# Loading the sampled blocks of V with plain transfers on SyncE instead of GpSimd's indirect gathers, in a block-sparse attention with feed-forward layer

## The chip, the cores and the metric

The kernel runs on one core of a Trainium2 chip. The core has five engines with an instruction stream each: TensorE (PE; its weight loads are listed apart as PEld), VectorE (DVE), ScalarE (ACT), GpSimd (POOL) and SyncE (SP), which here only issues transfers. Sixteen DMA engines move the data between the device's memory (HBM) and the core's memory (SBUF). A transfer is issued by SP or ACT (a plain one) or by POOL (here: an indirect one, whose rows are given by a list of indices in SBUF). The metric is the device time of one execution in microseconds (us), as a median of several runs.

## What is computed

Attention over 4 batches, 8 heads, 768 positions and head size 64, followed by a feed-forward layer with softplus. The positions are cut into 24 blocks of 32. A query block sees its own key block and the two beside it, the first and the last block, and three sampled blocks that are given as data; the first and the last query block see everything.

```
blk_i, blk_j = pos[:, None] // 32, pos[None, :] // 32
mask = np.abs(blk_i - blk_j) <= 1
mask |= (blk_i == 0) | (blk_j == 0) | (blk_i == 23) | (blk_j == 23)
for qb in range(24):
    for kb in sampled_blocks[qb]:
        mask[qb*32:(qb+1)*32, kb*32:(kb+1)*32] = True
scores = np.where(mask, scale * q @ k.T, -1e9)
x = softmax(scores) @ v
h = x @ w_in
out = softplus(h) @ w_out
```

The sampled blocks are the same for all batches and heads.

## The kernel before

Each batch has six sets of query blocks. A set is four query blocks (two in the last), worked on in two units of four heads each; one more set per batch, the whole one, holds the first and the last query block, which see all keys. The sets go through the stages scores (L581), exponents (L642), transposes (L661), values (L682), normalise, turn, x_high and x_low. The pieces of three neighbouring units are interleaved (L768).

For the values of a set, `load_values` (L533) fills one of two buffers `vbuf` ("vg" in the profile). SP loads the neighbouring blocks of all query blocks with one transfer (L549) and, where the first and last block aren't in the buffer yet, those too (L558, L561). The three sampled blocks of each query block are one indirect transfer on POOL (L567): 96 rows of 512 floats, chosen by a column of the index table `ix`. There are 22 such gathers per batch, 88 in all. A set's gathers aren't issued at once: they are put on the list `value_work`, and `gather` (L460) takes one from it, and one from the list `key_work`, after every piece of attention; `gathered` empties the list of what a set needs before its value products.

The sampled key blocks take another way. The keys of a batch stand in SBUF, and POOL (for the very first set DVE and ACT) copies each sampled block to its place at an address from a register (L511). Its number comes out of a register into which the packed block numbers `pk` have been read (`registers`, L451; the read is L454). `pk` holds three numbers of five bits per query block, two query blocks to a 32-bit word.

At the start DVE makes the index table and the packed numbers from the sampled blocks (`make_index` L385 with the conversions L386 and L387, L391 and L396, then `pack_blocks` L375 to L383), then the mask. PE runs 100 warm-up matmuls (L831) meanwhile.

The order of instructions: SP's is that of the program, word for word. DVE's is so while `make_index` to the first keys are traced, POOL's for the first gathers. All else is ordered by a planner from estimated costs, except single instructions that are kept behind everything traced before them on their engine, such as ACT's two steps on each half of the weights (L155, L159).

Other things on SP, in its order around `load_values`: the queries of a set two further on (`load_queries`, L447, "qc"); the halves of the feed-forward weights as 64-bit numbers (L148, "raw"), which ACT (L155, L159), DVE (L165, L172, L178) and POOL (L182) turn into 32-bit floats; those halves that don't stay in SBUF, written back (L201, "wD"); the attention's result for the second pass over the layer (L766, "xD") and the partial results of the first pass (L317, "yD"); the keys of the next batch (L431, "kT").

In the program's text the start is: block numbers, queries 0, keys 0, warm-up, index and mask, queries 1, values of set 0, values of set 1, queries 2, the first three halves of the weights. The feed-forward matmuls (L237 to L239 and L295 to L297) of the first pass fill PE beside the attention from the fourth set on; those of the second pass come after it.

Of the kernel before, what the change touches and what calls it, by code (L numbers as in the profile page):

```python
# [8 lines left out]
F32 = mybir.dt.float32  # L9
F32R = mybir.dt.float32r  # L10
I32 = mybir.dt.int32
# [4 lines left out]
ALU = mybir.AluOpType  # L16
# [3 lines left out]
BLOCK = 32  # L20
# [30 lines left out]
def sparse_attention_ffn(  # L51
# [22 lines left out]
    nc = tc.nc  # L74
    B, NG, P, NP, NI, _ = q.shape
    NB = k.shape[2]
    S = NB * BLOCK
    LAST = NB - 1
# [7 lines left out]
    NR = 3  # L86
# [243 lines left out]
    ac = actx.enter_context(tc.tile_pool(name="ac", bufs=1, side="right"))  # L330
# [4 lines left out]
    rf = ac.tile([P, NB, NR], F32, name="rf")  # L335
    pkf = ac.tile([1, NB], F32, name="pkf")
    pk = ac.tile([1, NB - 2], I16, name="pk")
    pk32 = pk.bitcast(I32)
    io = ac.tile([NR * BLOCK, 1], I32, name="io")
    first = ac.tile([P, 1], I32, name="first")  # L340
    iof = ac.tile([NR * BLOCK, 1], F32, name="iof")
    ixf = ac.tile([NR * BLOCK, NB], F32, name="ixf")
    ix = ac.tile([NR * BLOCK, B, NB], I32, name="ix")
    mask = ac.tile([P, NG, NS], F32, name="mask")
    iu = ac.tile([P, NG], I32, name="iu")
    iuf = ac.tile([P, NG], F32, name="iuf")
# [5 lines left out]
    for i in range(NI):  # L352
        nc.gpsimd.iota(
            iu[i * BLOCK : (i + 1) * BLOCK], pattern=[[NI, NG]], base=1 + i, channel_multiplier=0
        )
    for s in range(NR):
        nc.gpsimd.iota(io[s * BLOCK : (s + 1) * BLOCK], pattern=[[0, 1]], base=0, channel_multiplier=1)
    for rows in (slice(0, NR * BLOCK), slice(NR * BLOCK, P)):
        nc.gpsimd.iota(first[rows], pattern=[[0, 1]], base=0, channel_multiplier=1)
    vbuf = [ac.tile([P, 2, NI, DM], F32, name=f"vg{n}") for n in range(2)]  # L360
# [2 lines left out]
        out=vbuf[0][:, 0, 0, :], out_offset=None, in_=v,  # L363
        in_offset=bass.IndirectOffsetOnAxis(ap=first, axis=0),
# [17 lines left out]
        )  # L382
        nc.vector.tensor_copy(out=pk, in_=pkf[:, 1 : NB - 1])  # L383

    def make_index():  # L385
        nc.vector.tensor_copy(out=iof, in_=io)  # L386
        nc.vector.tensor_copy(out=rf, in_=blk.rearrange("p (i s w) -> p i s w", s=NR, w=2)[:, :, :, 0])  # L387

        for s in range(NR):
            rows = slice(s * BLOCK, (s + 1) * BLOCK)  # L390
            nc.vector.tensor_scalar(  # L391
                out=ixf[rows], in0=rf[rows, :, s], scalar1=float(BLOCK), scalar2=iof[rows, 0:1],
                op0=ALU.mult, op1=ALU.add,
            )
        for b in range(B):
            nc.vector.tensor_scalar_add(out=ix[:, b], in0=ixf, scalar1=float(b * S))  # L396

    def make_mask():
        nc.vector.tensor_copy(out=iuf, in_=iu)
# [51 lines left out]
    def registers(eng, us):  # L451
        for u in us:
            if (eng, u) not in regs:
                regs[eng, u] = eng.value_load(pk32[0:1, u : u + 1], min_val=0, max_val=(1 << 31) - 1)  # L454
        return [regs[eng, u] for u in us]


    key_work, value_work = [], []

    def gather():  # L460
        for work in (value_work, key_work):
            if work:
                work.pop(0)[1]()

    def gathered(work, m):
        while work and work[0][0] <= m:
            work.pop(0)[1]()
# [17 lines left out]
    def gather_keys(m):  # L485
        b, g = order[m]
        ni = NI if g < NG - 1 else 2
        kd = kg[m % 2]

        def of_block(i):  # L490

            eng = (nc.vector if i < 2 else nc.scalar) if m == 0 else nc.gpsimd
            copy = nc.scalar.copy if m == 0 and i >= 2 else eng.tensor_copy
            if i == 0:
                at = kT[b][:, 4 * g : 4 * g + NR, :]
                pattern = [list(x) for x in at.ap]
                ins = nc.vector.tensor_copy(
                    out=kd[:, 0:ni, 0:NR, :].rearrange("p i s f -> p i (s f)"),
                    in_=bass.AP(at.tensor, at.offset, [pattern[0], [NP * BLOCK, ni], [1, NR * NP * BLOCK]]),
                )  # L500
                tc.keep_in_program_order(ins)
                if m % NG < 2:
                    first = nc.vector.tensor_copy if m == 0 else nc.scalar.copy
                    end_keys(m, (first, nc.scalar.copy))
            (r,) = registers(eng, [2 * g + i // 2])
            for s in range(NR):
                x = nc.s_assert_within(
                    eng.snap((r >> (16 * (i % 2) + 5 * s)) & 31), 0, LAST,
                    skip_runtime_bounds_check_because="a sampled block is one of the key blocks",
                )  # L510
                copy(  # L511
                    out=kd[:, i, 1 + NR + s, :], in_=kT[b][:, bass.ds(x, 1), :].rearrange("p n f -> p (n f)")
                )

        key_work.extend((m, lambda i=i: of_block(i)) for i in range(ni))


# [15 lines left out]
    def load_values(m):  # L533
        if m >= len(sets):
            return
        b, g, whole = sets[m]
        vd = vg[sets[m]] = vbuf[m % 2]
        if whole:
            rows = vd.rearrange("p c i f -> p (c i) f")
            for n in range(0, NCH, 2):  # L540
                lo = b * S + n * P
                nc.sync.dma_start(
                    out=rows[:, n : n + 2], in_=v[lo : lo + 2 * P].rearrange("(t p) f -> p t f", p=P)
                )
            return
        ni = NI if g < NG - 1 else 2

        i0 = 1 if m == 0 else 0
        nc.sync.dma_start(  # L549
            out=vd[0 : 3 * BLOCK, 0, i0:ni], in_=overlapping(v, b * S + (4 * g + i0) * BLOCK, ni - i0, 3 * BLOCK)  # L550
        )
        if g < 2:

            for c, lo in enumerate((b * S, (b + 1) * S - BLOCK)):
                i1 = i0 if c == 0 else 0
                if m < SPREAD:
                    if i1 == 0:
                        nc.sync.dma_start(out=vd[3 * BLOCK : P, c, 0], in_=v[lo : lo + BLOCK])  # L558
                    spread.append((vd[3 * BLOCK : P, c, 0:1], vd[3 * BLOCK : P, c, 1:]))
                    continue  # L560
                nc.sync.dma_start(  # L561
                    out=vd[3 * BLOCK : P, c, i1:],
                    in_=v[lo : lo + BLOCK].unsqueeze(1).to_broadcast([BLOCK, NI - i1, DM]),
                )

        def of_block(i):
            nc.gpsimd.indirect_dma_start(  # L567
                out=vd[0 : 3 * BLOCK, 1, i, :],
                out_offset=None,
                in_=v,  # L570
                in_offset=bass.IndirectOffsetOnAxis(ap=ix[:, b, 4 * g + 1 + i : 4 * g + 2 + i], axis=0),
            )

        value_work.extend((m, lambda i=i: of_block(i)) for i in range(ni))


    units = [(m, a) for m in range(len(sets)) for a in range(NA)]
# [104 lines left out]
    def values(n):  # L682
        m, a = units[n]
        b, g, whole = sets[m]
        pt = state[n]["pt"]
        gathered(value_work, m)
        vd = vg[sets[m]]
        if a == 0:
            xps[m] = ps_x.tile([P, DM], F32, tag="x", name=f"x{n}")
        xq = xps[m]  # L690

        if not whole:
            ni = NI if g < NG - 1 else 2
            for j in range(2):
                for r in range(2):
                    h = 2 * (2 * a + j) + r
                    for c in range(2):
                        for i in range(ni):
                            rows = slice(i * BLOCK, (i + 1) * BLOCK)
                            nc.tensor.matmul(  # L700
                                xq[rows, h * D : (h + 1) * D],
                                pt[r, 2 * j + c][:, rows],
                                vd[:, c, i, h * D : (h + 1) * D],
                                start=(c == 0), stop=(c == 1),
                            )
        else:
            rows_v = vd.rearrange("p c i f -> p (c i) f")
            for r in range(2):
                at = (2 * a + r) * D
                for c in range(NCH):  # L710
                    for o in range(2):
                        rows = slice(64 * o, 64 * o + 64)
                        h = 2 * (2 * a + o) + r
                        nc.tensor.matmul(  # L714
                            xq[rows, at : at + D],
                            pt[r, c][:, rows],
                            rows_v[:, c, h * D : (h + 1) * D],
                            start=(c == 0), stop=(c == NCH - 1),
                        )
# [110 lines left out]
    for n in range(WARM):  # L830
        nc.tensor.matmul(warm[:, n % 4], ident, ident, start=True, stop=True)  # L831
    with tc.manual_schedule(engines={mybir.EngineType.DVE}):
        make_index()
        pack_blocks()
        make_mask()
        load_keys(0)
        gathered(key_work, 0)
# [2 lines left out]
    load_keys(1)  # L840
    scores(0)
    with tc.manual_schedule(engines={mybir.EngineType.Pool}):
        gathered(value_work, 0)
        gathered(key_work, 1)
    spread_ends()
    load_values(1)
# [69 lines left out]
    for j in range(len(seq) + LEAD):  # L916
        if j >= SECOND:
            t, f = seq[j][1:] if j < len(seq) else (NTB, -1)
# [62 lines left out]
```

## Time and profile before

| What | Value |
|---|---|
| Median of 3 runs | 808.4 us (807.98 to 809.11) |
| Profiled execution, first to last instruction | 812.1 us |
| PE busy | 781.7 us |
| DVE busy | 574.8 us |
| ACT busy | 489.6 us |
| POOL busy | 223.3 us |
| Mean granted clock of PE | 0.989 |
| Bytes moved by DMA | 129.65 MB, of these 17.57 MB on POOL's queue |

The profile gives the span from the first to the last instruction of one execution; no other time is given for that execution. The span is 3.7 us longer than the median of the runs without a profile. "Idle before, releaser" is the time an engine stood before an instruction and what ended it; "issue" means that nothing in the profile explains it. SPq, ACTq, DVEq and POOLq are the instruction queues of the engines: transfers, register operations and semaphores, which aren't counted as busy. In a timeline a row is start, duration, engine, line, operation, destination and source, and how many instructions were merged.

### The profile page before, as it was taken

What the parts mean: (1) busy time and instruction counts of PE and PEld (TensorE: products, weight loads), DVE (VectorE), ACT (ScalarE), POOL (GpSimd) and SP (SyncE); (2) the same over time, 40 slices, a digit from 0 to 9 for tenths busy, and PEclk for the clock granted to TensorE, in tenths of its full rate; (3) what the DMA queues carried; (4) which work ended last, traced back from release to release, by engine and by line L of the source; (5) the groups of instructions that cost most, each with busy time, mean ns of one, the idle gap of its engine ahead of it and who ended that gap; (6) DMA issues with size and microseconds to landing.
All of it is one profiled execution on the core that took longest, in us unless ns stands there. A gap on an engine that the chain in (4) does not pass through costs nothing.

```text
span 812.1 us, 21433 instructions
## 1 busy us (share of the span) xinstructions
PE 781.7 (96%) x8108; PEld 647.6 (80%) x8108; DVE 574.8 (71%) x1474; ACT 489.6 (60%) x1182; POOL 223.3 (27%) x389
## 2 busy tenths in 40 slices
PE   8878898999999999999999999999999999999997
PEld 8545676877677777778778988999988999988996
DVE  5778999876887777886655985656565656656564
ACT  5878785757767767767565764444444444444442
POOL 6864775635565436563000000000000000000000
PEclk9999898999999999999999999999999999999999
DMA  8899678687696777866425640304040312122021
GB/s 254 241 257 336 171 212 266 195 294 247 184 291 198 248 261 200 267 171 184 158 78 182 250 178 20 137 1 155 2 146 10 116 40 105 52 88 68 0 79 40
DMA packets 48408, 129.65 MB, mean 160 GB/s; under 512 B 5489, under 2 KB 5617, under 8 KB 46257
## 3 DMA queue, kind: packets, MB, share of 16 engines
q1 hardware_dynamic: 42304, 109.79, 42.3%
q0 software_dynamic: 5712, 17.57, 7.6%
q8 instruction: 64, 1.05, 0.5%
q10 hardware_dynamic: 288, 0.93, 0.3%
q14 instruction: 40, 0.32, 0.1%
HBM read 97.85 MB, written 30.41 MB: 158 GB/s over the span
## 4 chain that ended last, share of the span: by engine, by line
PE 82%; DVE 7%; ACT 6%; DMA 2%; issue 2%; POOL 0%; SPq 0%; ACTq 0%; DVEq 0%; POOLq 0%
PE o L295 11%; PE h L237 11%; PE o L297 10%; PE o L296 10%; PE h L238 10%; PE h L239 10%; PE s L601 5%; PE t L670 4%; PE x L700 4%; ACT pr L657 3%; PE warm L831 2%; DMA kT<-in_k_dram 1%; PE s L625 1%; DVE pr L607 1%; PE x L714 1%
## 5 line engine op out<-in xcount | busy, mean ns | idle before, releaser
L237 PE MATMUL h<-x,w 128*128 128x384 f32 x512 | 180.0, 352 | 0.4 <-DVE nmax L632 0.2
L238 PE MATMUL h<-x,w 128*128 128x384 f32 x512 | 173.7, 339 | 0.0
L239 PE MATMUL h<-x,w 128*128 128x384 f32 x512 | 173.1, 338 | 0.0
L250 DVE TENSOR_SCALAR u<-e 128x384 f32<-128x384 f32 x128 | 50.8, 397 | 155.8 <-ACT e L244 154.4
L295 PE MATMUL o<-w,gh 128*128 128x512 f32 x384 | 158.7, 413 | 0.0
L657 ACT ACTIVATE pr<-pr,nmax 128x256 f32<-128x256 f32 (+2 forms) x208 | 110.4, 532 | 74.6 <-DVE nmax L607 60.4
L297 PE MATMUL o<-w,gl 128*128 128x512 f32 x384 | 152.0, 396 | 1.2 <-issue 1.0
L296 PE MATMUL o<-w,gh 128*128 128x512 f32 x384 | 151.7, 395 | 0.0
L243 ACT ACTIVATE e<-h 128x384 f32<-128x384 f32 x128 | 62.4, 487 | 114.9 <-PE h L239 114.8
L267 ACT CAST gh<-u 128x384 fp32r<-128x384 f32 x128 | 65.6, 513 | 79.2 <-PE o L296 78.1
L237 PEld LDWEIGHTS h<-x,w 128*128 128x128 f32 x512 | 96.6, 189 | 19.4 <-issue 11.2
L567 POOL DMA_INDIRECT vg<-in_v_dram,ix x88 | 90.3, 1027 | 65.9 <-PE x L700 39.1
L238 PEld LDWEIGHTS h<-x,w 128*128 128x128 f32 x512 | 96.8, 189 | 6.5 <-issue 2.2
L511 POOL COPY kg<-kT 128x128 f32 x252 | 86.0, 389 | 41.2 <-PE s L601 38.8
L239 PEld LDWEIGHTS h<-x,w 128*128 128x128 f32 x512 | 96.6, 189 | 0.0
L295 PEld LDWEIGHTS o<-w,gh 128*128 128x128 f32 x384 | 72.0, 188 | 19.9 <-issue 7.1
L297 PEld LDWEIGHTS o<-w,gl 128*128 128x128 f32 x384 | 72.1, 188 | 18.8 <-issue 1.5
L296 PEld LDWEIGHTS o<-w,gh 128*128 128x128 f32 x384 | 72.2, 188 | 10.3 <-issue 0.4
L607 DVE CUSTOM_DVE_ANT_1 pr<-s,mask 128x256 f32<-128x256 f32 (+1 forms) x192 | 69.6, 414 | 14.5 <-PE s L601 14.5
L258 ACT ACTIVATE u<-u 128x384 f32<-128x384 f32 x128 | 66.9, 523 | 15.4 <-DVE e L252 15.2
L263 DVE TENSOR_TENSOR u<-u,e 128x384 f32<-128x384 f32 x128 | 73.6, 575 | 3.0 <-ACT u L258 2.4
L273 DVE TENSOR_TENSOR gl<-u,gh 128x384 fp32r<-128x384 f32 x128 | 73.0, 570 | 2.8 <-ACT gh L267 2.8
(81 smaller groups left out, 1088.6 us busy)
## 6 DMA issues: line engine op xcount, KB each, us to landing
vg<-in_v_dram SPq DMA_DIRECT2D x19, 768.0 KB, 5.8
xD<-x SPq DMA_DIRECT2D x8, 1536.0 KB, 7.4
x<-xD SPq DMA_DIRECT2D x8, 1536.0 KB
raw<-in_w_in_dram SPq DMA_DIRECT2D x16, 512.0 KB, 9.3
raw<-in_w_out_dram SPq DMA_DIRECT2D x16, 512.0 KB, 8.3
qc<-in_q_dram SPq DMA_DIRECT2D x24, 256.0 KB, 6.9
vg<-in_v_dram SPq DMA_DIRECT2D x12, 512.0 KB, 7.4
yD<-os SPq DMA_DIRECT2D x24, 256.0 KB, 2.5
```

What stands on the lines that cost most here:

```text
L237: nc.tensor.matmul(ph, wh[:, cols], hi[:, c], start=(c == 0), stop=False)
L238: nc.tensor.matmul(ph, wh[:, cols], lo[:, c], start=False, stop=False)
L239: nc.tensor.matmul(ph, wl[:, cols], hi[:, c], start=False, stop=(c == NC - 1))
L263: nc.vector.tensor_tensor(out=l, in0=l, in1=e, op=ALU.add)
L273: nc.vector.tensor_tensor(out=gl, in0=l, in1=G[n].bitcast(F32), op=ALU.subtract)
L295: nc.tensor.matmul(po[m], gh[:, cols], wh, start=first, stop=False)
L296: nc.tensor.matmul(po[m], gh[:, cols], wl, start=False, stop=False)
L297: nc.tensor.matmul(po[m], gl[:, cols], wh, start=False, stop=last)
L511: copy(out=kd[:, i, 1 + NR + s, :], in_=kT[b][:, bass.ds(x, 1), :].rearrange("p n f -> p (n f)"))
L567: nc.gpsimd.indirect_dma_start(out=vd[0 : 3 * BLOCK, 1, i, :], out_offset=None, in_=v, in_offset=bass.IndirectOffsetOnAxis(ap=ix[:, b, 4 * ...
L607: nc.vector.tensor_tensor_reduce(out=pr[r][rows, j], in0=ps[r][rows, j], in1=mask[rows, g].unsqueeze(2).to_broadcast([ni * BLOCK, NS, BLOCK]),
L657: nc.scalar.activation(x, x, AF.Exp, bias=nmax[rows, r, j : j + 1], scale=-1.0, accum_out=rs[rows, h : h + 1])
```

## The change

Each sampled block of V is loaded by SP as a plain transfer of 32 rows of 512 floats (64 KB, contiguous in HBM), at an address that SP works out in registers from the packed block numbers. Three transfers per query block take the place of one gather: 264 for 88. They are issued in `load_values` itself, right behind the set's other loads, and are no longer spread over the pieces of attention. SP reads `pk` into registers (11 reads, at the first use of each). The index table, its tiles and the instructions that made it are gone; `make_index` becomes `read_blocks`, and only converts the block numbers. The extraction of a block number from its word is now one function for keys and values.

```
-    for s in range(NR):
-        nc.gpsimd.iota(io[s * BLOCK : (s + 1) * BLOCK], pattern=[[0, 1]], base=0, channel_multiplier=1)
...
-    def make_index():
-        nc.vector.tensor_copy(out=iof, in_=io)
+    def read_blocks():
         nc.vector.tensor_copy(out=rf, in_=blk.rearrange("p (i s w) -> p i s w", s=NR, w=2)[:, :, :, 0])
-
-        for s in range(NR):
-            rows = slice(s * BLOCK, (s + 1) * BLOCK)
-            nc.vector.tensor_scalar(
-                out=ixf[rows], in0=rf[rows, :, s], scalar1=float(BLOCK), scalar2=iof[rows, 0:1],
-                op0=ALU.mult, op1=ALU.add,
-            )
-        for b in range(B):
-            nc.vector.tensor_scalar_add(out=ix[:, b], in0=ixf, scalar1=float(b * S))
...
+    def sampled(eng, r, i, s):
+        return nc.s_assert_within(
+            eng.snap((r >> (16 * (i % 2) + 5 * s)) & 31), 0, LAST,
+            skip_runtime_bounds_check_because="a sampled block is one of the key blocks",
+        )
+
+    v_blocks = v.rearrange("(n p) f -> n p f", p=BLOCK)
...
     def gather():
-        for work in (value_work, key_work):
-            if work:
-                work.pop(0)[1]()
+        if key_work:
+            key_work.pop(0)[1]()
...
-        def of_block(i):
-            nc.gpsimd.indirect_dma_start(
-                out=vd[0 : 3 * BLOCK, 1, i, :],
-                out_offset=None,
-                in_=v,
-                in_offset=bass.IndirectOffsetOnAxis(ap=ix[:, b, 4 * g + 1 + i : 4 * g + 2 + i], axis=0),
-            )
-
-        value_work.extend((m, lambda i=i: of_block(i)) for i in range(ni))
+        for i in range(ni):
+            (r,) = registers(nc.sync, [2 * g + i // 2])
+            for s in range(NR):
+                nc.sync.dma_start(
+                    out=vd[s * BLOCK : (s + 1) * BLOCK, 1, i, :],
+                    in_=v_blocks[bass.ds(sampled(nc.sync, r, i, s) + b * NB, 1)].rearrange("n p f -> (n p) f"),
+                )
...
-        gathered(value_work, m)
```

More of the change, by code (lines that the diff above doesn't have):

```diff
@@ L338, in sparse_attention_ffn @@
     pk32 = pk.bitcast(I32)
-    io = ac.tile([NR * BLOCK, 1], I32, name="io")
     first = ac.tile([P, 1], I32, name="first")
-    iof = ac.tile([NR * BLOCK, 1], F32, name="iof")
-    ixf = ac.tile([NR * BLOCK, NB], F32, name="ixf")
-    ix = ac.tile([NR * BLOCK, B, NB], I32, name="ix")
     mask = ac.tile([P, NG, NS], F32, name="mask")
@@ L455, in registers @@
         return [regs[eng, u] for u in us]
-    key_work, value_work = [], []
+    def sampled(eng, r, i, s):
[4 more added lines that the diff above has]
+    v_blocks = v.rearrange("(n p) f -> n p f", p=BLOCK)
+    key_work = []
     def gather():
-        for work in (value_work, key_work):
-            if work:
-                work.pop(0)[1]()
+        if key_work:
+            key_work.pop(0)[1]()
     def gathered(work, m):
@@ L506, in of_block @@
             for s in range(NR):
-                x = nc.s_assert_within(
-                    eng.snap((r >> (16 * (i % 2) + 5 * s)) & 31), 0, LAST,
-                    skip_runtime_bounds_check_because="a sampled block is one of the key blocks",
-                )
+                x = sampled(eng, r, i, s)
                 copy(
@@ L564, in load_values @@
                 )
-        def of_block(i):
-            nc.gpsimd.indirect_dma_start(
-                out=vd[0 : 3 * BLOCK, 1, i, :],
-                out_offset=None,
-                in_=v,
-                in_offset=bass.IndirectOffsetOnAxis(ap=ix[:, b, 4 * g + 1 + i : 4 * g + 2 + i], axis=0),
-            )
-        value_work.extend((m, lambda i=i: of_block(i)) for i in range(ni))
+        for i in range(ni):
[5 more added lines that the diff above has]
+                )
     units = [(m, a) for m in range(len(sets)) for a in range(NA)]
@@ L832, in sparse_attention_ffn @@
     with tc.manual_schedule(engines={mybir.EngineType.DVE}):
-        make_index()
+        read_blocks()
         pack_blocks()
@@ L842, in sparse_attention_ffn @@
     with tc.manual_schedule(engines={mybir.EngineType.Pool}):
-        gathered(value_work, 0)
         gathered(key_work, 1)
```

## The prediction

> **What bounds the kernel now.** I read the windows first, to see in which stage TensorE (PE) has idle time at all, then the waits of PE, then the timelines of SP, ACT and PE where the idle time is.
>
> ```profile
> PE 781.7 (96%) x8108; PEld 647.6 (80%) x8108; DVE 574.8 (71%) x1474; ACT 489.6 (60%) x1182; POOL 223.3 (27%) x389
> 15.00:60.00 45.00, 35.12 (x856) 23.55 (x855) 33.13 (x112) 37.33 (x103) 35.23 (x67) 0.96 0.92 249
> 60.00:140.00 80.00, 69.85 (x995) 51.15 (x995) 75.05 (x187) 59.13 (x152) 50.73 (x73) 0.91 0.83 254
> 140.00:480.00 340.00, 335.27 (x4537) 264.45 (x4536) 258.96 (x724) 235.70 (x610) 128.17 (x221) 1.00 0.67 211
> 480.00:812.10 332.10, 327.94 (x1633) 294.92 (x1631) 199.51 (x410) 151.99 (x309) 0.00 (x0) 1.00 0.20 68
> ```
>
> Each window row gives its length, then busy us of PE, weight loads, DVE, ACT and POOL, the granted clock, the DMA share and GB/s. From 140 us on PE is idle for only 4.7 of 340 us and 4.2 of 332 us, at a granted clock of 1.00: it is the bound there, and what goes on beside it costs nothing unless it is later than PE's order allows. In the first 140 us PE is idle for 9.9 and 10.2 us of the two early windows. There the chain of work runs through ACT and DVE, and DMA is 0.92 and 0.83 busy. So the change is decided in the first sets of attention, and by whether anything becomes late afterwards.
>
> How much of PE's idle time do the gathers cause today?
>
> ```profile
> L567 POOL DMA_INDIRECT vg<-in_v_dram,ix x88 | 90.3, 1027 | 65.9 <-PE x L700 39.1
>   DMA vg<-in_v_dram,ix: 2.4, 4
> PEld s L601 <- POOL kg L511: 0.5, 2, 0.4
> 43.02 0.42 PE L700 MATMUL x<-vg,pt 128*32 128x64 f32 x12
> 43.92 0.30 PE L700 MATMUL x<-vg,pt 128*32 128x64 f32 x2 [0.48 <-DMA vg<-in_v_dram,ix]
> 44.75 0.97 PE L700 MATMUL x<-vg,pt 128*32 128x64 f32 x50 [0.53 <-DMA vg<-in_v_dram,ix]
> ```
>
> The gathers take 90.3 us of POOL, but POOL is busy for 27% of the span. The value products wait 2.4 us for gathers in all (weight loads and matmuls counted each, so about 1.2 us of real time: the pauses of 0.48 and 0.53 us at 43 to 45 us are nearly all of it). The scores wait 0.5 us for key copies on POOL. What can be won directly is thus 1.7 us.
>
> **The change part by part.** *Removed:* 88 gathers on POOL: 90.3 us of an engine off the path; worth the 1.2 + 0.5 us above. Eight small DVE instructions of the index:
>
> ```profile
> 6.63 0.71 DVE L391 TENSOR_SCALAR ixf<-rf,iof 32x24 f32<-32x24 f32 x3
> 7.37 0.42 DVE L396 TENSOR_SCALAR ix<-ixf 96x24 int32<-96x24 f32 x4
> 8.12 0.17 DVE L383 CAST pk<-pkf 1x22 int16<-1x22 f32 x1
> 1.45 14.28 PE L831 MATMUL warm<-ident 128*128 128x128 f32 x100 [1.45 <-POOL ident masks.py:199]
> ```
>
> They bring the packed block numbers `pk` from 8.29 to about 7.2 us, and everything behind them on DVE forward by 1.1 us. PE is in its warm-up until 15.73 us, which hides this: 0. Without that cover it would be worth the 1.1 us.
>
> *Added:* 264 transfers of 64 KB on SP, three per query block, with their register work, and a read of `pk` on SP.
>
> ```profile
> 189.11 1.75 SPq L431 DMA_DIRECT2D kT<-in_k_dram  x4
> L558 SPq DMA_DIRECT2D vg<-in_v_dram x3: 322/322/802, 2.8 to 10.1; - x3
> L511 ACTq ALU_OP  x11: 38/38/44, 12.2 to 13.4; - x11
> L511 ACTq FUSED_REGOPS  x6: 46/46/52, 12.3 to 13.5; - x6
> L454 ACTq TENSOR_LOAD <-pk x1: 473/473/473, 11.4 to 11.4; - x1
> L454 POOLq TENSOR_LOAD <-pk x11: 283/291/499, 8.3 to 21.8; - x11
> out_dram<-y SPq DMA_DIRECT2D x4, 64.0 KB, 2.1
> SPq L558 <- DMA kT<-in_k_dram: 3.9, 1, 3.9
> ```
>
> No transfer with a register address stands in this trace. SP issues four plain ones in 1.75 us, 0.44 us each. The key copies get their block number by two register operations of 38 ns and one of 46 ns; batches after the first add one more of 38 ns. That makes 0.60 us; I take **0.65 us**, nearest to the plain row. The low end is 0.44 us (register work hidden), the high end 0.80 us (the one 32 x 2 KB transfer that took 802 ns) plus 0.16, 0.96 us. A set of four blocks thus holds SP for 12 x 0.65 = 7.8 us, and in the first batch two register loads of about 0.46 us more. 64 KB alone lands in 2.1 us.
>
> There is a second limit. The eight transfers issued before 5.95 us (six on SP, two on ACT) all go at once; the ninth and tenth stand until the first ones, `qc` and `kT`, have landed (3.9 us of SP for `kT`). SP has eight in flight, no more, so a gather also waits for the one eight places ahead. The Trainium skill, page "DMA: Bandwidth & Descriptors", section "Issuing engines are not separate DMA queues", says that starting transfers on several engines saves only the sequencer's time. By that rule this second limit would be absent, and the start-up sum below would be about 1 us smaller (gathers back to back from 7.9 us end at 16.2, not 17.1); the 3.9 us row is against it.
>
> *Moved:* everything behind the gathers in SP's fixed order. That is the cost.
>
> ```profile
> 3.60 0.60 SPq L549 DMA_DIRECT2D vg<-in_v_dram  x1
> 5.95 4.52 SPq L558 DMA_DIRECT2D vg<-in_v_dram  x2
> 18.21 2.10 SPq L148 DMA_DIRECT2D raw<-in_w_in_dram  x3
> 38.46 0.34 SPq L549 DMA_DIRECT2D vg<-in_v_dram  x1
> 38.85 1.50 SPq L447 DMA_DIRECT2D qc<-in_q_dram  x1
> 20.99 1.31 PE L700 MATMUL x<-vg,pt 128*32 128x64 f32 x64
> 33.31 1.10 PE L700 MATMUL x<-vg,pt 128*32 128x64 f32 x64
> 28.21 0.67 ACT L155 ACTIVATE wt<-raw 128x512 f32<-128x512 f32 x1
> 52.47 1.09 PE L601 MATMUL s<-kg,qc 64*32 64x256 f32 x32
> 145.04 0.33 SPq L549 DMA_DIRECT2D vg<-in_v_dram  x1
> 167.46 1.10 PE L700 MATMUL x<-vg,pt 128*32 128x64 f32 x64
> L148 SPq DMA_DIRECT2D raw<-in_w_in_dram x16: 327/406/1411, 18.2 to 301.4; - x16
> DMA to landing us min/median/max: 3.5/9.1/13.4
> L447 SPq DMA_DIRECT2D qc<-in_q_dram x24: 328/458/1802, 0.7 to 375.6; - x24
> DMA to landing us min/median/max: 5.5/6.9/9.3
> ```
>
> Start-up: SP reaches the gathers of set 0 at 4 us and stands until `pk` (7.2) is there and loaded (7.9). Numbers four to eight then wait for the large first loads; the twelfth goes out near 16.5 us (18.5 if the eight-in-flight wait is at its worst), lands by 18.6 (20.6), and the first value products start at 20.99: hidden, by a margin of 0.4 to 2.4 us. Then the three loads of set 1 (1.5 us, to 18.6), twelve gathers and two register loads (8.7 us, to 27.4; landed 29.5, needed 33.31, hidden), `qc`, and the first weight load at **27.9 us instead of 18.21**. It lands 3.5 us later at the best, 31.4 us. ACT's first step on it, L155, runs at 28.21, ahead of the exponents of the fourth unit; ACT is busy for 37 of 45 us here and PE waits for its exponents. Cost: 31.4 - 28.2 = **+3.2 us**. By the ends: at 0.44 us the load goes out 5 us earlier and the cost is 0; at 0.96 us it goes out 7.4 us later and the cost is 10.6.
>
> Later sets: a buffer is released at 38.46, and SP then goes 0.34 + 0.9 + 7.8 + 0.45 us before the next `qc` is out, 9.5 us, instead of 0.9. Landing takes 3 to 5.5 us (256 KB behind an emptied queue, by 64 KB in 2.1 at the one end, the shortest `qc` of before at the other). The scores that need it start at 52.47, 14.0 us after the release: 12.5 to 15.0 us against 14.0, so 0 to 1.0 us at each of about four such places: **+1.0**, bounds 0 and 4. From 140 us on a buffer released at 145.04 is read again at 167.46, 22 us later; its gathers land after about 11 (0.34 + 7.8 + 2.1, and up to 1 us of other loads): hidden under PE's work on the set between. Even at 0.96 us a gather this takes 15 us, and the cover holds.
>
> Sum: +3.2 + 1.0 - 1.2 - 0.5 = **+2.5 us**. The profiled execution spans 812.1 us, 3.7 more than the median 808.4 of the runs; I set the difference against the median: **810.9 us**.
>
> **The rivals.** *Hidden anyway (808.2).* ACT's order comes from a planner. Should it put the fourth unit's exponents ahead of the late L155, the 3.2 us go to the weight conversion alone, which no exponent waits for. Left: +1.0 - 1.2 - 0.5, and some part of a microsecond for the later weights. For it: exponents don't depend on weights. Against it: L155 does stand ahead of them now.
>
> *Faster (804.6).* POOL's order is the true limit between 30 and 50 us.
>
> ```profile
> 48.59 1.46 POOL L511 COPY kg<-kT 128x128 f32 x6
> 49.85 0.64 PE L601 MATMUL s<-kg,qc 64*32 64x256 f32 x8 [2.11 <-issue]
> ```
>
> PE stands 2.11 us at 47.7 to 49.85 with no releaser named, and goes on as six copies of POOL end that stood behind its gathers. If that pause hangs on POOL, it goes too: -1.2 - 0.5 - 2.1 = -3.8 us, and nothing is given back if a gather costs under 0.5 us of SP, the point from which this decides, as the first weight load is then in time. The Trainium skill, page "SBUF — State Buffer", section "Who interferes with whom", has VectorE and GpSimd lock each other out of a shared port, with SP's transfers free of it; no row here shows a gather holding up VectorE, and no number hangs on it. Against this rival: the copies need no value data, and the wait lists give POOL 0.5 us.
>
> *SP becomes the bound (818).* From 0.9 us a gather on, a set takes SP 12.5 us with its other work (12 x 0.9, 0.34, 0.9, 0.45), of the 14.0 us between release and scores, and the first weights land 6 us later than in the forecast: +9.2, four times about 0.8, less 1.7, is +10 us; at 0.96 us and with the worse landings about +12. For it: the one transfer of this shape at 802 ns. Against it: the other two of that line took 322.
>
> **How the numbers follow.** Forecast 0.35 (own range 809.8 to 814), hidden 0.26, faster 0.25, SP-bound 0.14. Within 0.2% is 1.6 us, about what can be told from no change here: faster 0.25, same 0.26, slower 0.35 + 0.14 = 0.49. The range, **804 to 819**, takes in the faster case's value and the SP-bound case's without its last part.
>
> **What would show it.** SP's gathers at a pace of 0.65 us; the first `raw` issue near 28 us instead of 18.21; ACT idle before L155 for about 3 us, released by the `raw` transfer; no PE wait for gathers at 43 to 45 us; POOL busy near 133 us; from 140 us on no more PE idle than 4.7 us. A pace under 0.5 us, exponents ahead of L155, or a lost pause at 47.7 us would make it wrong on the one side, a pace near 0.9 us on the other.

## The result, and the profile after

The changed kernel takes **867.26 us** (median of 4 runs, 865.99 to 871.16); the kernel before took 808.75 us beside it (807.98 to 810.48). The ratio is 1.0716, 95% interval 1.0686 to 1.0746. The prediction was 810.9 us, at most 819. Here and below, slower executions are left out (one each of e8 and e13). The profiled execution spans 864.5 us instead of 812.1, at a mean granted clock of 0.975 instead of 0.989.

In the profile after, line numbers have moved: the gathers are L557, the neighbour load L537 (was L549), the other set loads L530 and L546, the value products L685 and L699 (was L700 and L714), scores L587 (L601), transposed probabilities L663 (L677), exponents L643, queries L431 (L447). L148 to L317 stay. First the busy times and the chain from the page, then the windows that the prediction used:

```profile
PE 807.3 (93%) x8108; PEld 656.4 (76%) x8108; DVE 576.1 (67%) x1466; ACT 490.4 (57%) x1182; POOL 139.8 (16%) x298
...
PE 73%; DVE 13%; ACT 10%; issue 2%; DMA 1%; POOL 0%; SPq 0%; ACTq 0%; DVEq 0%; POOLq 0%
```

```profile
15.00:60.00 45.00, 32.49 (x706) 21.39 (x704) 27.53 (x94) 31.06 (x88) 18.07 (x47) 0.81 0.68 184
60.00:140.00 80.00, 68.39 (x1018) 49.36 (x1017) 66.52 (x179) 57.84 (x147) 33.70 (x55) 0.96 0.79 237
140.00:480.00 340.00, 312.59 (x4369) 230.34 (x4368) 233.68 (x666) 209.02 (x557) 82.61 (x173) 0.97 0.65 192
480.00:864.50 384.50, 380.30 (x1923) 341.87 (x1921) 241.79 (x494) 187.13 (x383) 0.00 (x0) 1.00 0.25 88
```

Most of the added idle time is not at the start, where I had looked for it: from 15 to 140 us PE is idle for 24.1 us instead of 20.0. From 140 to 480 us PE is idle for 27.4 us (340 less 312.59) where it had been for 4.7. Over the whole span PE is idle for 57.2 us instead of 30.4, and its busy time is 25.6 us longer for the same 8108 matmuls; the two make up the 52.4 us between the spans. The granted clock is lower as well (0.81 instead of 0.96 in the first window); no run here holds it fixed, so its share in the busy time stays open.

Who ended PE's waits, and how SP stood? Each row of the wait lists gives engine and line, what it waited for, us in total, times, and the longest.

```profile
SPq L537 <- PE x L685: 66.5, 11, 16.1
SPq L557 <- DMA vg<-in_v_dram: 35.4, 31, 3.0
PEld o L295 <- ACT gh L267: 18.6, 12, 2.3
PE o L295 <- ACT gh L267: 15.9, 12, 2.2
PE x L685 <- ACT pt L663: 7.7, 4, 6.5
PEld x L685 <- issue: 25.9, 76, 1.9
```

PE waits above all for `gh`, the hidden layer's output from ACT, ahead of the feed-forward's second product (L295). L295 has no such wait in the trace of before. Transfers are 1% of the chain. So the trace after does not accuse SP: in 11 places SP itself still stands, for 66.5 us, until PE releases a value buffer. The gathers' stops for earlier value transfers (35.4 us in 31) are new, but PE's value products wait only 3.2 us for transfers.

Two theories follow. **R, run time:** SP's longer queue brings queries, weights and value blocks late on the chip. **O, order:** SP now has 264 transfers, and the planner, which orders all engines but SP from estimated costs, has laid PE, ACT, DVE and POOL out otherwise; that order costs the time, whether the data are late or not.

### The profile page after: what moved, and what is told of

Same layout as the page of the kernel before. It is cut to its first block, busy times and chain, and to the rows that moved or that the text cites. A ratio compares the mean times of both kernels' runs of the same rounds, so it can differ in the third digit from the quotient of the medians.

```text
span 864.5 us, 22676 instructions
## 1 busy us (share of the span) xinstructions
PE 807.3 (93%) x8108; PEld 656.4 (76%) x8108; DVE 576.1 (67%) x1466; ACT 490.4 (57%) x1182; POOL 139.8 (16%) x298
## 2 busy tenths in 40 slices
DMA packets 55457, 129.75 MB, mean 150 GB/s; under 512 B 8304, under 2 KB 8432, under 8 KB 53296
## 4 chain that ended last, share of the span: by engine, by line
PE 73%; DVE 13%; ACT 10%; issue 2%; DMA 1%; POOL 0%; SPq 0%; ACTq 0%; DVEq 0%; POOLq 0%
PE o L297 10%; PE o L295 10%; PE o L296 10%; PE h L237 9%; PE h L238 9%; PE h L239 9%; PE s L587 5%; PE x L685 4%; ACT pr L643 4%; PE t L656 3%; DVE pr L593 2%; DVE e L252 1%; DMA kT<-in_k_dram 1%; DVE kg L488 1%; DVE wt L178 1%
## 5 line engine op out<-in xcount | busy, mean ns | idle before, releaser
L295 PE MATMUL o<-w,gh 128*128 128x512 f32 x384 | 155.7, 406 | 17.0 <-ACT gh L267 15.9
L297 PE MATMUL o<-w,gl 128*128 128x512 f32 x384 | 155.7, 409 | 1.9 <-DVE gl L273 1.9
L643 ACT ACTIVATE pr<-pr,nmax 128x256 f32<-128x256 f32 (+2 forms) x208 | 110.2, 532 | 65.1 <-DVE nmax L593 57.2
L250 DVE TENSOR_SCALAR u<-e 128x384 f32<-128x384 f32 x128 | 47.6, 372 | 130.7 <-ACT e L244 130.4
L499 POOL COPY kg<-kT 128x128 f32 x252 | 92.5, 413 | 118.7 <-PE s L587 109.8
L295 PEld LDWEIGHTS o<-w,gh 128*128 128x128 f32 x384 | 73.1, 191 | 32.7 <-ACT gh L267 18.6
L685 PEld LDWEIGHTS x<-vg,pt 128*32 128x32 f32 x2816 | 52.9, 112 | 45.9 <-issue 25.9
L296 PEld LDWEIGHTS o<-w,gh 128*128 128x128 f32 x384 | 73.2, 191 | 14.3 <-issue 0.9
L685 PE MATMUL x<-vg,pt 128*32 128x64 f32 x2816 | 70.3, 226 | 14.8 <-ACT pt L663 7.7
L273 DVE TENSOR_TENSOR gl<-u,gh 128x384 fp32r<-128x384 f32 x128 | 76.0, 595 | 10.2 <-ACT gh L267 10.1
```

Source lines behind the costliest of these rows:

```text
L273: nc.vector.tensor_tensor(out=gl, in0=l, in1=G[n].bitcast(F32), op=ALU.subtract)
L295: nc.tensor.matmul(po[m], gh[:, cols], wh, start=first, stop=False)
L296: nc.tensor.matmul(po[m], gh[:, cols], wl, start=False, stop=False)
L297: nc.tensor.matmul(po[m], gl[:, cols], wh, start=False, stop=last)
L499: copy(out=kd[:, i, 1 + NR + s, :], in_=kT[b][:, bass.ds(x, 1), :].rearrange("p n f -> p (n f)"))
L643: nc.scalar.activation(x, x, AF.Exp, bias=nmax[rows, r, j : j + 1], scale=-1.0, accum_out=rs[rows, h : h + 1])
```

## The experiments

All times are medians, in us; the ratio is to the kernel before in the same group of runs, with its 95% interval.

| Run | What it is | Time | Before beside it | Ratio |
|---|---|---|---|---|
| e1 | changed, all four engines in the order of before | 841.18 | 810.27 | 1.0365 (1.0309 to 1.0421) |
| e2 | before, all four engines in the changed order | 863.80 | 810.27 | 1.0668 (1.0635 to 1.0701) |
| e3 | changed, PE alone in the order of before | 838.88 | 810.27 | 1.0354 (1.0322 to 1.0386) |
| e4 | changed, all but PE in the order of before | 855.27 | 810.27 | 1.0563 (1.0525 to 1.0601) |
| e5 | e1, gathers spread over the pieces | 825.36 | 834.02 | |
| e6 | e1, gathers ahead of the neighbour load | 842.78 | 834.02 | |
| e7 | e1, one broadcast transfer for three (the second and third sampled block left out) | 907.22 | 834.02 | |
| e8 | e1, fixed blocks instead of the sampled ones, no register work | 825.71 | 834.02 | |
| e1b | e1 again | 838.05 | 829.47 | |
| e5b | e5 again | 825.63 | 829.47 | |
| e9 | e1, gathers behind the queries | 838.04 | 829.47 | |
| e10 | e5 without a held order | 883.27 | 829.47 | |
| e11 | e1, a third of the transfers from the third set on (the others left out) | 809.72 | 809.11 | 1.0018 (0.9993 to 1.0043) |
| e12 | e5 and e8 in one | 818.94 | 809.11 | 1.0123 (1.0076 to 1.0170) |
| e13 | before, PE alone in the changed order | 860.20 | 809.11 | 1.0645 (1.0572 to 1.0718) |
| e14 | before, one run | 806.75 | 809.11 | |
| e15 | changed, gathers spread, PE in program order | 818.02 | 811.71 | 1.0079 (1.0057 to 1.0101) |
| e5c | e5 again | 824.72 | 811.71 | 1.0175 (1.0150 to 1.0200) |

In two groups (e5 to e10) the kernel before took 834.02 and 829.47 us and not 809 to 812, for a cause that was not found, so their ratios are left out. The kernels without gathers on POOL repeat across groups (e5: 825.36, 825.63, 824.72; e1: 841.18, 838.05) and are compared with each other.

### Order or run time: e1 to e4 and e13

The order of an engine is held by chaining its instructions, each behind the one ahead of it, with an edge that fixes the order of issue and adds no wait for data. The list is that of the other kernel. SP stays in program order throughout.

```
     with _tile.TileContext(nc) as tc, tc.manual_schedule(engines={_mybir.EngineType.SP}):
         sparse_attention_ffn(tc, *args)
+        hold(tc, list(nc.cur_bb.bb.instructions))
...
+        for a, b in zip(order, order[1:]):
+            tc.add_manual_dep(b, a.name, dep, reason="held")
```

Expected of e1:

> The changed kernel, with the instructions of TensorE, ScalarE and VectorE and the copies and subtractions of GpSimd held in the order that they have in the kernel before. SP's gathers stay as changed. Theory R (run time: SP's longer queue of 12 gathers a set brings qc, weights and values late on the chip, whatever the order): stays at 867, at least above 855. Theory O (order: the planner laid the four engines' work out in another order because of the gathers, and that order costs the time): falls to 809, within 805 to 815; what remains above 808.75 is the true price of the longer queue, which my prediction had at +2.5 us.

Of e2:

> The kernel before, gathers on GpSimd, with TensorE, ScalarE, VectorE and GpSimd's copies and subtractions held in the changed kernel's order; no gather on SP. Theory R: stays at 809 (805 to 815). Theory O: rises to 860 to 870, since the order alone carries the loss. In between (825 to 850) both take part.

Of e3 (the list of PE alone) and e4 (the lists of the other three):

> The changed kernel with TensorE alone held in the order of before; the planner orders the other three round it. Theory R: 867. Theory O, if TensorE's order (feed-forward products drawn in among value products and ahead of their ScalarE input) is what costs: 809 to 825. If the order of ScalarE or VectorE is what costs: above 845.

> The changed kernel with ScalarE, VectorE and GpSimd's copies held in the order of before; TensorE alone is left to the planner. Theory R: 867. Theory O with TensorE's order as the carrier: still above 845. With the order of the other engines as the carrier: 809 to 825.

And of e13, run later:

> The kernel before, gathers on GpSimd, with TensorE alone held in the order of the changed kernel; the planner orders the others round it. If TensorE's order carries e2's loss: within 10 us of e2 (1.055 to 1.07 of the kernel before). If ScalarE's or VectorE's order does: under 1.03.

Neither theory holds alone. The changed order, with the gathers still on POOL and landing in time (the value products wait 1.3 us for them, 1.0 before), costs 863.80 - 810.27 = 53.5 us (e2); PE's order alone, with the other engines ordered round it by the planner, costs 860.20 - 809.11 = 51.1 us (e13). The longer queue, with the order of before, costs 841.18 - 810.27 = 30.9 us (e1; I had it at 2.5). Together they cost 58.5, not 84: they overlap. Taking PE's changed order away from the changed kernel gains 28 us (e3), the other engines' orders 12 (e4). e1 and e3 fell between the bands of the two theories, since each had left the other's cost out.

What the order does is seen in PE's timeline of e13 (start, duration, instruction, idle before and who ended it), in the stage in which the kernel before did 64 value products in one block of 1.10 us (the row at 167.46 in the prediction):

```profile
156.87 0.41 PE L700 MATMUL x<-vg,pt 128*32 128x64 f32 x10
159.10 0.50 PE L295 MATMUL o<-w,gh 128*128 128x512 f32 x1 [1.82 <-ACT gh L267]
...
161.06 0.30 PE L700 MATMUL x<-vg,pt 128*32 128x64 f32 x2
...
162.31 0.50 PE L295 MATMUL o<-w,gh 128*128 128x512 f32 x1 [0.29 <-ACT gh L267]
...
164.64 0.50 PE L297 MATMUL o<-w,gl 128*128 128x512 f32 x1 [1.37 <-DVE gl L273]
165.07 0.30 PE L700 MATMUL x<-vg,pt 128*32 128x64 f32 x2
...
166.66 0.75 PE L700 MATMUL x<-vg,pt 128*32 128x64 f32 x36
...
168.95 0.42 PE L700 MATMUL x<-vg,pt 128*32 128x64 f32 x14
```

The 64 products between two whole blocks come in five pieces (10, 2, 2, 36, 14) that take 2.18 us in all (1.91 us without their overlap with the next matmul, against 1.03 for the one block), between feed-forward products that stand 3.5 us here for `gh` and `gl`, not yet computed. The value blocks aren't late; the order is. Both losses stand in e13's groups by line (busy us and mean ns of one, then idle us before them); those of before follow:

```profile
L295 PE MATMUL o<-w,gh 128*128 128x512 f32 x384 | 155.4, 406 | 14.5 <-ACT gh L267 14.5
...
L297 PE MATMUL o<-w,gl 128*128 128x512 f32 x384 | 155.7, 409 | 7.7 <-DVE gl L273 7.7
...
L700 PE MATMUL x<-vg,pt 128*32 128x64 f32 x2816 | 69.6, 225 | 9.8 <-ACT pt L677 5.3 <-ACT wt L155 2.4 <-issue 0.9
```

```profile
L295 PE MATMUL o<-w,gh 128*128 128x512 f32 x384 | 158.7, 413 | 0.0
L297 PE MATMUL o<-w,gl 128*128 128x512 f32 x384 | 152.0, 396 | 1.2 <-issue 1.0
...
L700 PE MATMUL x<-vg,pt 128*32 128x64 f32 x2816 | 55.4, 223 | 5.3 <-ACT pt L677 3.9 <-DMA vg<-in_v_dram,ix 1.0 <-issue 0.4
```

One value product lasts 225 ns instead of 223, yet their busy time grows from 55.4 to 69.6 us: in short runs they overlap each other less (the ends of matmuls are modelled in the profile). PE waits 14.5 us for `gh` and 7.7 for `gl`, where it had waited for neither. These 36 us (14.2 + 14.5 + 7.7) are most of the 46.0 us between e13's span, 858.1, and that of before.

### What the queue costs: e1, e9, e6, e11

With the order of before, SP's queue gets into the chain of work that ended last. The page gives that chain for the kernel before and for e1:

```profile
PE 82%; DVE 7%; ACT 6%; DMA 2%; issue 2%; POOL 0%; SPq 0%; ACTq 0%; DVEq 0%; POOLq 0%
```

```profile
PE 74%; DMA 15%; SPq 4%; ACT 2%; DVE 2%; issue 2%; DVEq 0%; ACTq 0%
```

Transfers and SP's issuing are 19% of it, where they were 2%. SP's queue in e1 (start, duration of the merged issues, line, transfer), PE's timeline at the same place, and SP's waits, of before and of e1:

```profile
237.02 0.97 SPq L537 DMA_DIRECT2D vg<-in_v_dram  x1
238.04 1.31 SPq L549 DMA_DIRECT2D vg<-in_v_dram  x2
239.61 13.36 SPq L557 DMA_DIRECT2D vg<-in_v_dram  x12
253.02 0.42 SPq L431 DMA_DIRECT2D qc<-in_q_dram  x1
253.48 0.42 SPq L201 DMA_DIRECT2D wD<-wt  x1
254.01 0.37 SPq L148 DMA_DIRECT2D raw<-in_w_in_dram  x1
254.48 0.42 SPq L751 DMA_DIRECT2D xD<-x  x1
255.02 0.41 SPq L537 DMA_DIRECT2D vg<-in_v_dram  x1
```

```profile
256.24 1.96 PE L587 MATMUL s<-kg,qc 64*32 64x256 f32 x32 [2.46 <-DMA qc<-in_q_dram]
```

```profile
SPq L549 <- PE x L700: 119.2, 17, 14.3
```

```profile
SPq L557 <- DMA vg<-in_v_dram: 49.0, 29, 4.1
SPq L537 <- PE x L685: 17.1, 5, 12.2
```

SP goes from one set's loads straight to the next's. The twelve gathers take 13.36 us here, 7.8 of them issue (12 by 0.65) and the rest stops until an earlier transfer has landed; behind them stand the queries, for which PE waits 2.46 us. Before, SP stood 119.2 us in 17 places waiting for a released buffer, 7.0 us each: that was its reserve. The gathers need at least 7.8 us a set, and in e1 the reserve is down to 17.1 us in 5 places. Of the 29.6 us between e1's span and that of before, 19.9 are idle time of PE and 9.7 longer busy time, at a mean granted clock of 0.969 instead of 0.989.

Is it the place ahead of the queries, the stops, or the number? First the place: e9 puts all twelve gathers behind the query load.

```
-        for i in range(ni):
+        def of_block(i):
             (r,) = registers(nc.sync, [2 * g + i // 2])
...
+        value_work.extend((m, lambda i=i: of_block(i)) for i in range(ni))
...
             if scored is not None:
                 load_queries(scored + 2)
+            gathered(value_work, len(sets))
```

> As e1, but the twelve gathers of a set, still in one go, are issued behind the next query load in place of ahead of it; nothing else moves. If late queries are what costs (TensorE waited 19.5 us for qc in e1, and ran at a granted clock of 0.81 to 0.83 from 15 to 100 us): 1.00 to 1.015 of the kernel before, with no wait of TensorE for qc. If late weights, neighbour rows or the stops behind large transfers are: 1.02 to 1.035.

TensorE's waits for the queries fell to 2.9 us, and the time stayed: 838.04 against 838.05. (Its bands are ratios to the kernel before, which took 829.47 in this group, and can't be used.) The queries were only what stood nearest. What is late in e9's trace are the keys of the next batch: ACT's waits for `kT` grow from 7.9 us in e1 to 16.6, DVE's from 8.8 to 17.6, and at 324.85 us PE has stood 7.20 us behind ACT, which had itself stood 7.42 us for `kT`. Spreading the gathers (e5: the list `value_work` emptied by `gather`, one block a piece, as the kernel before did) gained 12.4 us against e1b:

> As e1 (changed kernel, the four engines held in the order of before), but SP's gathers are handed out one block at a time over the pieces of attention that follow, as GpSimd's were, instead of all twelve behind the neighbour load: the next queries and weights stand ahead of most of them in SP's fixed order. If it is the place ahead of queries and weights that cost e1 its 31 us: 809 to 816, TensorE's waits for qc (19.5 us in e1) gone. If the count of transfers or their pace costs, wherever they stand: 830 to 841.

> e5 once more (gathers handed out one block at a time over the attention pieces, engines held in the order of before). If the place of the gathers ahead of queries and weights costs e1 its loss: at most 1.012 of the kernel before on this chip, and at least 2% under e1b. If number or pace of the transfers costs wherever they stand: within 1% of e1b.

e5 lies between its two bands. Of e5b, the first bound was met (0.9958), but only since the kernel before took 829.47 in that group: beside 811.71 the same kernel stands at 1.0175 (e5c). The second, 2% under e1b, was missed, with 1.5%. Place is a part of the 31 us, under half. e6 asked about the stops, by moving the loop over the gathers up:

```
+        for i in range(ni):
+            (r,) = registers(nc.sync, [2 * g + i // 2])
...
         i0 = 1 if m == 0 else 0
         nc.sync.dma_start(
             out=vd[0 : 3 * BLOCK, 0, i0:ni], in_=overlapping(v, b * S + (4 * g + i0) * BLOCK, ni - i0, 3 * BLOCK)
```

> As e1, but each set's twelve gathers are issued ahead of its neighbour load of 768 KB instead of behind it; queries and weights stay behind both. If the gathers' stops for the big load to land (SP stood 49.0 us in 29 of them in e1) are what costs: 810 to 822, and those stops go to under 15 us. If twelve gathers ahead of the queries cost by their own issue time of 7.9 us a set: above 830.

The stops for value transfers fell from 49.0 to 14.0 us, the time did not (842.78). But the first neighbour load then stood behind gathers that need the block numbers: it went out at 17.44 us, and not at 2.17 as in the changed kernel, and PE's busy time from 15 to 60 us fell to 23.60, from 31.39 in e1. So e6 says nothing certain of the stops. e11 leaves transfers out:

```
-            for s in range(NR):
+            for s in range(NR if m < 2 else 1):
```

> As e1, but from the third set on only the first of the three transfers a block is issued: 104 transfers in place of 264 (two thirds of the sampled rows of the later sets are left out). A set then holds SP 2.6 us and has four transfers behind its neighbour load. If the number of transfers on SP is what costs from the third set on: 815 to 825, the loss at the start (15 to 60 us) left, and SP's stops behind the neighbour loads, 47.1 us in e1b, under 10. If something else of e1 costs (clock, weights): above 832.

```profile
SPq L537 <- PE x L685: 89.0, 18, 13.1
...
SPq L557 <- DMA vg<-in_v_dram: 1.1, 1, 1.1
```

With 104 transfers for 264 the whole 31 us are gone, SP's reserve is back at 89.0 us in 18 places, and the stops are 1.1 us. The number, the issue time, the stops and the bytes (119.19 MB for 129.75) fall together here. The bytes alone are not it, as the kernel before moves 129.65 MB, a part of them on POOL's queue; the others e11 does not part. I had expected the start's loss to remain (815 to 825). It doesn't: in e11 the first two sets are loaded as in e1, the first weights go out at 31.02 us and PE is idle for 13.6 us from 15 to 60 (9.9 in the kernel before), and yet the kernel ends level.

### Pace, and a transfer that is dearer: e8, e12, e7

```
-                    in_=v_blocks[bass.ds(sampled(nc.sync, r, i, s) + b * NB, 1)].rearrange("n p f -> (n p) f"),
+                    in_=v_blocks[b * NB + 4 * g + i : b * NB + 4 * g + i + 1].rearrange("n p f -> (n p) f"),
```

> As e1, but the 264 transfers read fixed blocks, with no register work (the sampled blocks are replaced by fixed ones). By the rows a gather then takes SP 0.36 us or so instead of 0.655, a set 4.4 instead of 7.9. If SP's pace is the cause: down by some 12 to 20 us, to 821 to 829. If the stops behind big transfers are the cause, they take up what the registers leave: 835 to 841.

e8 (825.71) is 12 to 15 us under e1 and e1b, within its first band: a shorter issue pays, so the register work is on the path (that e8 reads one block three times is not parted from it), although SP's stops grew to 65.0 us as the gathers ran into them sooner. e12 joins it with e5:

> e5 (gathers spread over the attention pieces) and e8 (fixed blocks, no register work; sampled blocks are replaced by fixed ones) in one. If place and pace each take a part of e1's loss, and the parts add: 811 to 818. If both take away the same part: 823 to 827, as each alone.

818.94 lies between the two bands, nearer to adding: place and pace each take some, and each takes less after the other.

e7 was meant as e11 is, and is a miss of its own kind:

```
+            nc.sync.dma_start(
+                out=vd[0 : NR * BLOCK, 1, i, :],
+                in_=v_blocks[bass.ds(sampled(nc.sync, r, i, 0) + b * NB, 1)].to_broadcast([NR, BLOCK, DM]),
+            )
```

> As e1, but one transfer a block in place of three: it copies the first sampled block to all three places, the same bytes into the buffer in 88 transfers instead of 264 (the other two sampled blocks are left out). A set then holds SP for some 2.6 us instead of 7.9 and has four transfers behind the neighbour load, under the eight in flight. If number of transfers is the cause: 808 to 815. If the bytes or the register addresses as such are: above 830.

At a third of the number it takes 907.22 us. SP's rows of e7 (after the count the shortest, median and longest issue in ns, then the first and last start in us):

```profile
L556 SPq DMA_DIRECT2D vg<-in_v_dram x88: 723/788/8005, 8.3 to 499.3; - x88
```

```profile
L431 SPq DMA_DIRECT2D qc<-in_q_dram x24: 340/2520/4891, 0.8 to 473.2; - x24
```

The new transfer holds SP for up to 8.0 us, and the query load behind it takes 2.52 us to issue; in e1b it took 0.42. PE waits 73.4 us for queries. The Trainium skill, page "DMA: Bandwidth & Descriptors", section "Rules for kernel authors", says that an outermost dimension under 16, such as a broadcast of three copies, confines a transfer to at most as many DMA engines. Three copies are outermost here and the slowness agrees, but the trace doesn't show on which engines a transfer ran, so this cause is not shown. e7 says nothing of the number of transfers.

### Undoing the loss: e10, e15, e14

e10 is e5 without the line that holds the order:

```
-        hold(tc, list(nc.cur_bb.bb.instructions))
```

> e5's edit without any order held: the planner orders the four engines itself round the spread gathers. If the planner loses whenever 264 transfers stand on SP: above e5b by over 2%, towards 1.05 to 1.07 of the kernel before. If it lost only because all twelve stood ahead of the queries: within 1% of e5b.

883.27: without a held order the same edit that gained 12 us loses 58 (against e5b). So it is not the place of the gathers alone that spoils the order; with the spread ones it is spoilt as well. e15 takes PE out of the planner's hands, in one line:

```
-    with _tile.TileContext(nc) as tc, tc.manual_schedule(engines={_mybir.EngineType.SP}):
+    with _tile.TileContext(nc) as tc, tc.manual_schedule(engines={_mybir.EngineType.SP, _mybir.EngineType.PE}):
```

> The changed kernel with two plain edits in place of a held order: the gathers handed out one block at a time over the attention pieces (as in e5), and TensorE's instructions left in program order, so that the planner orders ScalarE, VectorE and GpSimd alone. If TensorE's order is the carrier of the 54 us and the spread takes a third of the queue's price: 1.00 to 1.025 of the kernel before, as e5c. If the other engines' order matters once SP's queue is long: over 1.035.

> e5 beside e15 and the kernel before in one call. Where the kernel before takes 809 or so: 818 to 826 (e12, with no register work, took 818.94 there), that is 1.01 to 1.02 of it. Where it takes 829 to 834: again 0.99 to 1.00. No version with all 264 transfers is expected to beat 809.

818.02 us: with two plain edits 49 of the 58 us are back, and it stands under e5c, whose order had been made for another queue. In its trace PE waits for neither `gh` nor `gl`, and is idle for 32.0 us (815.9 less 783.9) where the kernel before was for 30.4. It still doesn't beat the kernel before, and where that took 809 to 812 no version that loads all sampled blocks on SP did.

e14 was to show why the kernel before took longer in two groups; in its own group it did not (809.11), and the question stays open. The record names the same two chips for the groups with 834.02 and 829.47 as for those with 811.71 and 809.11, so it is not the chip alone.

> The kernel before, unedited, for its trace on a chip on which it may be slow (829 to 834 on two chips, 808 to 810 on the others, while e1 took 838 to 841 on both kinds). If the chips differ by GpSimd's indirect gathers: their landing is longer or GpSimd's mean over 1.0 us, and TensorE waits for them more than 1 us. If by the memory as a whole: SP's loads land later too. On a chip of the first kind: the page that is known.

## Why the prediction was wrong

*Step by step.* **The pace** was right: 0.65 us forecast. In the trace after, twelve gathers that meet hardly a stop take 7.99 us, 0.67 each, and the most frequent spacing of two issues is 0.65. First the rows of SP's part of L557 (registers, a move, the issue itself; gaps make up the rest), then those twelve:

```profile
L557 SPq ALU_OP  x484: 32/37/50, 8.1 to 464.7; - x162
L557 SPq FUSED_REGOPS  x264: 37/46/51, 8.2 to 465.1; - x132
L557 SPq MOVE vg<-in_v_dram x264: 29/29/37, 8.3 to 465.2; - x132
L557 SPq DMA_DIRECT2D vg<-in_v_dram x264: 315/316/1585, 8.4 to 465.2; - x132
```

```profile
160.50 7.99 SPq L557 DMA_DIRECT2D vg<-in_v_dram  x12
```

**The start** was right in its first step and wrong in the second. The first weights went out at 30.01 us (forecast 27.9), but ACT did not stand for them: its idle time before L155 is 0.0, where the sum had 3.2. The planner had put the fourth unit's exponents ahead of L155, which is what the rival "hidden anyway" had asked for; with the order of before held, ACT does stand for the weights, 3.24 us in e1 and 5.07 in e11. What PE waited for was the other thing that I had moved and not followed, the end blocks of set 1 (L546): ACT copies them onwards, stood 3.92 us for them, and the exponents came late behind it:

```profile
25.19 2.84 ACT L519 COPY vg<-vg 32x1536 f32<-32x1536 f32 x2 [3.92 <-DMA vg<-in_v_dram]
```

```profile
30.65 0.66 PE L685 MATMUL x<-vg,pt 128*32 128x64 f32 x16 [6.48 <-ACT pt L663]
...
48.54 1.28 PE L685 MATMUL x<-vg,pt 128*32 128x64 f32 x36 [1.40 <-DMA vg<-in_v_dram]
```

The second row also refutes the sign "no PE wait for gathers at 43 to 45 us": there is one of 1.40 us a little later. With all that, e11 puts the start's price and the gains together at -0.6 to +3.5 us (0.9993 and 1.0043 of 809.11), if leaving two thirds of the later blocks out gains nothing by itself; the sum had 3.2 - 1.2 - 0.5 = 1.5. By that, this term did not fail by its size.

**The later sets** failed: "+1.0, bounds 0 and 4", and "hidden under PE's work on the set between" from 140 us on. The queue costs 30.9 us (e1). I had followed one set through the queue and taken the pace alone; the stops behind eight transfers in flight, which I had priced at the start, I left out of every later set, where they stretch twelve gathers from 7.8 to between 10.0 and 17.45 us (e1, from 60 us on). And I asked whether one buffer's gathers land in time, not whether SP has 7.8 us to spare in each of its rounds; its wait row said 7.0. How the 30.9 us divide between issue and stops is not shown: e6 failed to part them, and e8, with a shorter issue, had longer stops. Nor is the limit of eight shown to be one of SP. In the trace the transfers of SP and ACT use eight semaphores in turn, and each waits on its own; so the program sets the limit, and the 3.9 us row can't tell whether SP has one.

**The SP-bound rival** had the mechanism and not its point: "from 0.9 us a gather on". e1 has the loss at 0.65, with the stops added. The price of 10 to 12 us was a third of what e1 shows, and too small by its own figures: with `qc` out 12.5 us after the release and 3 to 5.5 us to land, the scores are 1.5 to 4.0 us late at each of the four places, not "about 0.8", which makes 13.5 to 23.5 us.

**The term that was missing** is the largest. The prediction kept the order of PE, ACT, DVE and POOL as it was, though it says itself that ACT's order comes from a planner. That order changed throughout: PE's list breaks off from the program's order in 49 places in the kernel before (the list that e1 holds) and in 471 in the changed one (e2's). PE's part of it alone costs 51.1 us (e13). "From 140 us on no more PE idle than 4.7 us" fell with it: 27.4. e15 gets 49 us back by keeping PE in program order and spreading the gathers. Which part of the change leads the planner to the new order, SP's transfers, the gathers missing on POOL or the missing index instructions, was not tried.

**Why 31 and 54 make 58:** under the changed order the attention's rounds are longer, and SP has its reserve again, 66.5 us in 11 places after against 17.1 in 5 in e1. So, by these rows, the other loss covers the queue's lateness; no run tests this.

## What to carry to other kernels

Before work is put on a queue, read that queue's own waits: compare its mean wait a round (here 119.2 us in 17, 7.0 us each) with the work to be added (here 7.8 us), and count stops for transfers in flight as work. Where a planner orders engines, a change on one queue can reorder all of them; compare the order of the busiest engine before pricing single waits, and separate the two by holding one kernel to the other's order. When a trace shows waits between engines that the change didn't touch, suspect the order and not the data.

## What was not expected of the hardware

Value products of 0.22 us each cost 1.10 us as 64 in a row and 2.18 us as five pieces between other matmuls (1.03 and 1.91 without the overlap with the next matmul), at a granted clock of 1.00 in both: in this kernel the busy time of PE depends on how its instructions are mixed. And a transfer's issue can be held up by the one ahead of it: behind e7's broadcasts the query load took 2.52 us to issue (median) for 0.42 in e1b.
